# Batch 0's key-value products in four 128x32 tiles instead of two of 128x64

## The chip, the cores and the metric

The kernel runs on one core of one Trainium2 chip. The metric is the device time of one execution in microseconds (us); less is better. TensorE is called PE here, as in the profile, and its weight loads PEld; VectorE is DVE, ScalarE ACT, GpSimd POOL and SyncE SP.

## The reference

Two blocks follow each other. The first is a linear attention with a polynomial feature map: 4 batches, 4 heads, 1088 tokens, 32 channels a head, float32.

```python
phi(x)[i*8+j] = (S1 @ x)[i] * (S2 @ x)[j]          # 64 features from 32 channels
kv  = sum over tokens of phi(k) outer v            # 64 x 32, for each batch and head
z   = sum over tokens of phi(k)                    # 64
out = (phi(q) @ kv) / (phi(q) @ z + 1e-6)
```

Its output, transposed to 4352 tokens by 128 channels, goes through `gelu(x @ w_in) @ w_out` with 2048 hidden channels (exact gelu). The change touches `kv` and `z` of the first batch alone.

## The kernel before

**Staging.** The attention of batch 0 is computed first and alone, in a prologue of about 16 us. From then on PE works on the two large products of the second block (`hidden`, L735, and `project` / `two_products`, L872 and L821), 8 chunks of 512 tokens and a last one of 256 for the remainders, and the attention of batches 1 to 3 is put between them at fixed steps. Every engine executes its instructions in the order of the program text: the last lines of the kernel chain each instruction to the one before it on the same engine.

**The prologue around the change.** A batch has 1024 main tokens, worked on as 8 sets of 128 (one token to a partition), and a remainder of 64. Heads are handled as two pairs: `c` is the pair, `r` the head within it. `key_features` (L395) computes the features of the keys: products into PSUM (L390), a copy by ACT (L403, L406), the outer product by DVE (L407), one quarter of it by POOL (L404). `widen_v` (L353, POOL) copies the values beside a column of ones, so that one product gives `kv` and `z`: 33 columns. `expand_products` (L557) computes the sketches of the queries on PE, ACT copies half of them (L564) and DVE multiplies (L569, two instructions).

Then come the functions of the change. `kv_first(ps, r, tokens)` sums the products of the main tokens of head `r` of both pairs into one PSUM bank, `kv_first_rem` adds the remainder. In both, the stationary operand is the 64 features of one head over 128 tokens, and the moving operand the 33 columns of the values: the head of pair `c` writes PSUM partitions `64c` to `64c+63`. A matmul in float32 is two passes, and each pass is one record of PE and one of PEld in the trace.

On PE the order is:

```python
kv_first(kv_bank, 0, (0, 1, 4, 5))      # L434, 8 matmuls, 16 records
key_turn_rem(0, banks[1], by_act)       # L341, transpose of the remainder's keys; ACT copies it (kT_rem, L343)
kv_first(kv_bank, 0, (2, 3, 6, 7))      # L434, 16 records
key_features_rem(0, banks[1])           # L416, waits for kT_rem; ACT copies (a_rem, L420), DVE multiplies (k_p_rem, L421)
kv_first(kv_bank, 1)                    # L434, 32 records
kv_first_rem(kv_bank)                   # L440, 8 records, waits for k_p_rem
```

After these, PE transposes the queries of chunk 1 (L341, into `w_ps`), ACT copies the bank to `kz` (L941) and the transposed queries to `qT` (L948), and PE computes the numerators and denominators (L670) from `kz`. On ACT two steps of a weight's conversion (`bits_low` L263, `bits_r` L287) lie between `a_rem` and `kz`; on DVE the two multiplications of L569 lie ahead of `k_p_rem`, and the weight's conversion (L276 to L300) behind it.

Batches 1 to 3 sum `kv` in another form (`kv_product`, L445): the 32 values of a head over 128 tokens are stationary, the 64 features moving, and the four heads write four groups of 32 PSUM partitions. `z_sum` uses the same line with a tile of ones (32 columns) as the stationary operand.

Of the kernel before, what the change touches and what calls it, by code (L numbers as in the profile page):

```python
# [16 lines left out]
def kernel(  # L17
# [18 lines left out]
    pe, dve, act, pool, sp = nc.tensor, nc.vector, nc.scalar, nc.gpsimd, nc.sync  # L36
    B, H, S, D = q.shape
    R = S1.shape[0]
    F = R * R
# [3 lines left out]
    NP = H // 2  # L43
# [7 lines left out]
    C = D + 1  # L51
# [185 lines left out]
    v_rem_aug = [big.tile([128, H, D if b else 2 * D], FP, name=f"v_rem_aug{b}") for b in range(B)]  # L237
# [4 lines left out]
    v_aug = [att.tile([128, NP, J, 2 * D], FP, name="sums") for r in range(2)]  # L242
# [107 lines left out]
    kT, k_p, k_p_rem = {}, {}, {}  # L350
# [74 lines left out]
    def flat(features):  # L425
        return features.rearrange("p i j -> p (i j)")

    def kv_first(ps, r, tokens=range(J)):

        for i in tokens:  # L430

            ch, t, one = i // 4, i // 2 % 2, i % 2
            for c in range(NP):
                pe.matmul(ps[c * F:(c + 1) * F, r * 2 * D:r * 2 * D + C], lhsT=flat(k_p[0, r][:, t, c * 4 + ch * 2 + one]),  # L434
                          rhs=v_aug[r][:, c, i, :C], start=(r == 0 and i == 0), stop=False, skip_group_check=True)

    def kv_first_rem(ps):
        for r in range(2):
            for c in range(NP):
                pe.matmul(ps[c * F:(c + 1) * F, r * 2 * D:r * 2 * D + C], lhsT=flat(k_p_rem[0][:, 2 * c + r]),  # L440
                          rhs=v_rem_aug[0][:, 2 * c + r, :C], start=False, stop=True, skip_group_check=True)

    def kv_product(ps, lhsT, features, h, part, start=False, stop=False):

# [464 lines left out]
    r = Rounding(SR)  # L909
# [15 lines left out]
    for i in range(2):  # L925
        query_features(0, i)
    kv_bank = out_bank()
    kv_first(kv_bank, 0, (0, 1, 4, 5))
    key_turn_rem(0, banks[1], by_act)
    kv_first(kv_bank, 0, (2, 3, 6, 7))  # L930
    key_features_rem(0, banks[1])
    kv_first(kv_bank, 1)
    kv_first_rem(kv_bank)
    w_in = [Rounding(w) for w in w_in_sb[:2]]
    w_in[0].low_words()
# [167 lines left out]
    for n in range(3, NCHUNK):  # L1103

        t = (n - 1) * NF
# [160 lines left out]
```

## Time and profile before

| what | value |
|---|---|
| median of 3 runs | 259.04 us (258.95 to 259.43) |
| the profiled execution's own time | 259.29 us |
| its span | 257.5 us |
| PE busy | 253.3 us, 98% of the span, 2333 records |
| PEld / DVE / ACT / POOL busy | 135.0 / 151.7 / 114.4 / 164.1 us |
| granted PE clock | 1.00 |
| L434, 64 records | 2.4 us busy |
| L440, 8 records | 0.4 us busy |

A row of the trace gives the start, the duration and the engine, then line, operation, output tile and input tiles, the tile of the array that a matmul uses (`128*64` is 128 rows by 64 columns, the number of columns being that of the stationary operand), the shape of what is written, and the number of records. Of several matmuls in a row the duration is from the first start to the last end; one record of 33 columns lasts about 0.22 us from start to end, but the next begins long before that.

### The profile page before, as it was taken

The numbers are of one execution on the slowest core, as the hardware profiler recorded it, in microseconds if no ns is written. First come the engines' busy times: TensorE is split into PE (matmuls) and PEld (weight loads), VectorE is DVE, ScalarE is ACT, GpSimd is POOL, SyncE is SP. The second block draws the span as 40 slices with busy tenths as digits, with TensorE's granted clock in tenths as the row PEclk, the third lists the DMA queues.
The fourth block names the chain that finished last, engine by engine and source line by source line (L and its number), as shares of the span: only waits on it lengthen the run. The fifth ranks groups of instructions, "written<-read, shape, count | busy, mean of one in ns | idle before, by whom it ended". The sixth has DMA issues, their size and how long they took to land.

```text
span 257.5 us, 5763 instructions
## 1 busy us (share of the span) xinstructions
PE 253.3 (98%) x2333; PEld 135.0 (52%) x2333; DVE 151.7 (59%) x317; ACT 114.4 (44%) x221; POOL 164.1 (64%) x173
## 2 busy tenths in 40 slices
PE   8999999999999999999999999999999999999995
PEld 6856444355444545444444455455544444445794
DVE  3886879969698987580178976399307000700330
ACT  3685767433635333533335332523444334433442
POOL 3503016799968788587758775787758777877300
PEclk9999999999999999999999999999999999999999
DMA  6479848820000101101000002000200200020020
GB/s 208 136 221 368 179 105 210 224 47 10 3 0 13 30 1 23 20 12 31 3 0 3 0 10 36 1 1 3 41 3 7 37 0 1 7 36 0 3 41 20
DMA packets 29082, 13.48 MB, mean 52 GB/s; under 512 B 21888, under 2 KB 27264, under 8 KB 29056
## 3 DMA queue, kind: packets, MB, share of 16 engines
q1 hardware_dynamic: 28624, 12.79, 20.2%
q8 instruction: 18, 0.29, 0.5%
q10 hardware_dynamic: 432, 0.33, 0.4%
q14 instruction: 8, 0.07, 0.1%
HBM read 10.88 MB, written 2.23 MB: 51 GB/s over the span
## 4 chain that ended last, share of the span: by engine, by line
PE 98%; DVE 1%; issue 0%; ACT 0%; DVEq 0%
PE h_ps L735 45%; PE o_ps L821 33%; PE o_ps L872 5%; PE w_ps L869 3%; PE w_ps L445 1%; PE w_ps L592 1%; PE w_ps L904 1%; PE w_ps L647 1%; PE o_ps L434 1%; PE h_ps L751 1%; PE w_ps L989 1%; PE w_ps L557 0%; PE w_ps L670 0%; DVE x_tok L693 0%; PE h_ps L341 0%; PE w_ps L341 0%
## 5 line engine op out<-in xcount | busy, mean ns | idle before, releaser
L735 PE MATMUL h_ps<-xT,w_in 128*64 128x512 f32 (+3 forms) x514 | 136.8, 576 | 0.0
L742 ACT ACTIVATE block<-h_ps 128x512 f32<-128x512 f32 (+1 forms) x128 | 73.0, 571 | 117.3 <-PE h_ps L735 115.3
L735 PEld LDWEIGHTS h_ps<-xT,w_in 128*64 128x64 f32 (+1 forms) x514 | 41.7, 142 | 30.6 <-issue 11.9
L821 PE MATMUL o_ps<-block,w_out 128*64 128x256 f32 x224 | 57.5, 379 | 0.0
L786 POOL TENSOR_TENSOR bits_low<-block 128x512 f32<-128x512 f32 x28 | 36.1, 1290 | 27.6 <-ACT block L742 27.6
L821 PEld LDWEIGHTS o_ps<-block,w_out 128*64 128x64 f32 x224 | 30.5, 137 | 38.1 <-issue 27.6
L787 POOL TENSOR_TENSOR bits_a<-block 128x512 f32<-128x512 f32 x28 | 35.7, 1276 | 11.8 <-ACT block L742 11.6
L836 DVE COPY sums<-o_ps 64x256 f32<-64x256 f32 x8 | 3.3, 417 | 60.6 <-PE o_ps L821 60.6
L789 POOL TENSOR_TENSOR bits_m<-block,bits_e 128x512 f32<-128x512 f32 x28 | 36.0, 1287 | 2.2
L788 POOL TENSOR_TENSOR bits_e<-bits_a,block 128x512 f32<-128x512 f32 x28 | 36.0, 1286 | 2.2
L821 PE MATMUL o_ps<-block,small 128*64 128x256 f32 x112 | 28.8, 379 | 0.0
L821 PE MATMUL o_ps<-bits_a,small 128*64 128x256 f32 x112 | 28.8, 379 | 0.0
L821 PE MATMUL o_ps<-bits_low,small 128*64 128x256 f32 x112 | 28.8, 379 | 0.0
L821 PE MATMUL o_ps<-bits_m,w_out 128*64 128x256 f32 x112 | 28.7, 379 | 0.0
L821 PEld LDWEIGHTS o_ps<-block,small 128*64 128x64 f32 x112 | 15.2, 137 | 17.9 <-issue 10.8
L821 PE MATMUL o_ps<-bits_e,small 128*64 128x256 f32 x112 | 17.0, 383 | 0.0
L872 PE MATMUL o_ps<-g,w_out 128*128 128x512 f32 (+1 forms) x34 | 16.5, 572 | 0.0
L821 PEld LDWEIGHTS o_ps<-bits_m,w_out 128*64 128x64 f32 x112 | 15.3, 137 | 0.0
L821 PEld LDWEIGHTS o_ps<-bits_a,small 128*64 128x64 f32 x112 | 15.2, 137 | 0.0
L821 PEld LDWEIGHTS o_ps<-bits_low,small 128*64 128x64 f32 x112 | 15.2, 137 | 0.0
L604 DVE STREAM_TRANSPOSE w_ps<-w_ps 128x512 f32<-128x512 f32 (+1 forms) x7 | 4.8, 687 | 17.1 <-ACT xT L658 12.7
L821 PEld LDWEIGHTS o_ps<-bits_e,small 128*64 128x64 f32 x112 | 7.6, 137 | 10.6 <-issue 8.8
(197 smaller groups left out, 303.3 us busy)
## 6 DMA issues: line engine op xcount, KB each, us to landing
block<-in_moe_w_in_dram SPq DMA_DIRECT2D x3, 512.0 KB, 9.9
block<-in_moe_w_out_dram SPq DMA_DIRECT2D x3, 512.0 KB, 10.4
k<-in_k_dram SPq DMA_DIRECT2D x12, 128.0 KB, 2.8
v<-in_v_dram SPq DMA_DIRECT2D x12, 128.0 KB, 3.1
q<-in_q_dram SPq DMA_DIRECT2D x24, 64.0 KB, 2.6
out_dram<-oT SPq DMA_DIRECT2D x21, 64.0 KB, 2.2
q_first<-in_q_dram SPq DMA_DIRECT2D x2, 256.0 KB, 3.9
v<-in_v_dram SPq DMA_DIRECT2D x2, 256.0 KB, 4.5
```

The source lines that it names most:

```text
L434: pe.matmul(ps[c * F:(c + 1) * F, r * 2 * D:r * 2 * D + C], lhsT=flat(k_p[0, r][:, t, c * 4 + ch * 2 + one]), rhs=v_aug[r][:, c, i, :C], s ...
L604: dve.transpose(out=tok, in_=ps[:, :, :H2])
L735: pe.matmul(ps[rows, :W], lhsT=w[:, rows], rhs=xT[n][:, :W], start=True, stop=True)
L742: act.activation(out=g_of[n, fi][:, :W], in_=ps[:, :W], func=ACT.Gelu)
L786: pool.tensor_sub(out=s[3], in0=a11, in1=a21)
L787: pool.tensor_add(out=s[1], in0=a21, in1=a22)
L788: pool.tensor_sub(out=s[2], in0=s[1], in1=a11)
L789: pool.tensor_sub(out=s[4], in0=a12, in1=s[2])
L821: pe.matmul(acc[n][bank][half * 64:(half + 1) * 64, col:col + HW], lhsT=fixed, rhs=moving, start=opens and e == 0 and name in "4715", stop ...
L836: dve.tensor_copy(out=N[lo, 0, one], in_=a0[lo, one])
L869: pe.matmul(o_of[n][i][:, :128], lhsT=g[:, i * 128:(i + 1) * 128], rhs=w_tile(w_out_sb, fi), start=first, stop=final)
L872: pe.matmul(o_of[n][:, cols], lhsT=w_tile(w_out_sb, fi), rhs=g[:, cols], start=first, stop=final)
```

## The change

Each matmul of `kv_first` and `kv_first_rem` is split in two. A new function `kv_quarters` loops over the pair `c` and over `half`: 32 of a head's 64 features are the stationary operand, the moving operand is the same 33 columns, and the output goes to PSUM partitions `64c + 32*half` and the 31 behind. So 36 matmuls of 128x64 become 72 of 128x32. What is computed, the bank, the accumulation and the order of the calls stay as they are. No instruction of another engine is added, removed or moved, and the places where PE waits for another engine are the same; all lines behind the new function are numbered 5 higher, and its matmuls all stand at L433.

```diff
+    def kv_quarters(ps, r, features, values, start, stop):
+
+        for c in range(NP):
+            for half in range(2):
+                rows = slice(c * F + half * F // 2, c * F + (half + 1) * F // 2)
+                pe.matmul(ps[rows, r * 2 * D:r * 2 * D + C], lhsT=flat(features(c))[:, half * F // 2:(half + 1) * F // 2],
+                          rhs=values(c), start=start, stop=stop, skip_group_check=True)
+
     def kv_first(ps, r, tokens=range(J)):
 
         for i in tokens:
 
             ch, t, one = i // 4, i // 2 % 2, i % 2
-            for c in range(NP):
-                pe.matmul(ps[c * F:(c + 1) * F, r * 2 * D:r * 2 * D + C], lhsT=flat(k_p[0, r][:, t, c * 4 + ch * 2 + one]),
-                          rhs=v_aug[r][:, c, i, :C], start=(r == 0 and i == 0), stop=False, skip_group_check=True)
+            kv_quarters(ps, r, lambda c: k_p[0, r][:, t, c * 4 + ch * 2 + one], lambda c: v_aug[r][:, c, i, :C],
+                        r == 0 and i == 0, False)
 
     def kv_first_rem(ps):
         for r in range(2):
-            for c in range(NP):
-                pe.matmul(ps[c * F:(c + 1) * F, r * 2 * D:r * 2 * D + C], lhsT=flat(k_p_rem[0][:, 2 * c + r]),
-                          rhs=v_rem_aug[0][:, 2 * c + r, :C], start=False, stop=True, skip_group_check=True)
+            kv_quarters(ps, r, lambda c: k_p_rem[0][:, 2 * c + r], lambda c: v_rem_aug[0][:, 2 * c + r, :C], False, True)
```

## The prediction

> **What bounds the kernel now.** I read the page's chain first, then the chain in the stretch of the change (8 to 12.5 us), then the timeline of that stretch by engine, and last the rows of the tile shapes. The page's chain by engine, and its pieces in the stretch (start, us, what):
>
> ```profile
> PE 98%; DVE 1%; issue 0%; ACT 0%; DVEq 0%
> ```
>
> ```profile
> 8.31 0.59 PE o_ps L434 x16
> 8.90 0.26 PE o_ps L341
> 9.16 0.59 PE o_ps L434 x16
> 9.75 0.22 PE o_ps L416 x4
> 9.97 0.91 PE o_ps L434 x32
> 10.88 0.35 PE o_ps L440 x8
> ```
>
> PE ends nearly everything, and the chain puts 0.59 + 0.59 + 0.91 + 0.35 = 2.44 us of it on the matmuls that change. Taken at its word, faster matmuls here shorten the kernel by what they save. The chain goes back from each step to the instruction ahead on PE where it sees no wait, so the timeline of the same stretch must say whether PE could have begun earlier:
>
> ```profile
> 8.34 1.07 ACT L564 COPY A_sb<-w_ps 128x512 f32<-128x512 f32 x2 [0.80 <-PE w_ps L557]
> 8.84 0.33 PE L341 MATMUL o_ps<-ident,k_rem 128*128 128x128 f32 x1
> 8.96 1.28 DVE L569 TENSOR_TENSOR q_pT<-A_sb,w_ps 128x512 f32<-128x512 f32 x2
> 9.30 0.28 ACT L343 COPY kT_rem<-o_ps 128x128 f32<-128x128 f32 x1
> 9.64 0.34 PE L416 MATMUL o_ps<-S,kT_rem 128*64 128x64 f32 x4
> 10.24 0.42 DVE L421 TENSOR_TENSOR k_p_rem<-a_rem,o_ps 128x256 f32<-128x256 f32 x1
> 10.80 0.43 PE L440 MATMUL o_ps<-v_rem_aug,k_p_rem 128*64 128x33 f32 x8
> 10.96 0.51 ACT L287 ACTIVATE bits_r<-bits_e,below 128x256 uint32<-128x256 uint32 x1 [0.42 <-DVE bits_e L276]
> 11.16 0.66 PE L341 MATMUL w_ps<-ident,q_first 128*128 128x128 f32 x4
> 11.38 0.20 ACT L941 COPY kz<-o_ps 128x66 f32<-128x66 f32 x1
> 11.74 0.67 PE L670 MATMUL h_ps<-kz,q_pT 64*64 64x33 f32 x32
> ```
>
> Two places are pinned by others. L416 begins at 9.64, 0.06 us after ACT's `kT_rem` ends (9.58); ACT takes that copy up only when L564 is through, though its input was ready at 9.17 (8.84 + 0.33). L440 begins at 10.80, 0.14 us after DVE's `k_p_rem` ends (10.66), and DVE had no gap before it: L569 runs from 8.96 to 10.24. L564 hangs on L557, ahead of the change. So PE reaches L440 little before it may start, and the matmuls of L434 are hidden, nearly without slack, beside ACT and DVE.
>
> **The pace of each shape.** Starts overlap, so a record's price is (duration of the group less one record) over the records less one.
>
> ```profile
> 8.25 0.66 PE L434 MATMUL o_ps<-sums,k_p 128*64 128x33 f32 x16
> 55.11 1.08 PE L445 MATMUL w_ps<-k_p,v 128*32 128x64 f32 x64
> L434 PEld LDWEIGHTS o_ps<-sums,k_p x64: 132/138/138, 8.2 to 10.6; 128*64 128x64 f32 x64
> L445 PEld LDWEIGHTS w_ps<-k_p,v x192: 110/110/110, 55.1 to 154.1; 128*32 128x32 f32 x192
> ```
>
> L434: (0.66 - 0.22)/15 = 29 ns; L445: (1.08 - 0.22)/63 = 13.7 ns. Over one round of the tiles, two in L434 and four in L445, that is 58 and 55 ns. A weight load grows by 28 ns from 32 to 64 columns, so about 0.85 ns a column: 64 columns are 54 ns, 32 are 27. Streaming costs the same (matmuls of 64, 128 and 256 columns last 219, 273 and 379 ns): 33 columns are 28 ns, 64 are 54. So a round of L434 is its 64-column weight load (54) and 4 ns more; a round of L445 is its 64-column stream. The changed form has the small side of both, 32 columns to load and 33 to stream: 28 plus 4 is 32 ns a round of four tiles, 8 ns a record. The shape is in no row. Its bounds: 7 ns (28 over four tiles, nothing more) and 29 ns, L434's own price, if four tiles help nothing. L445 is the nearest row, the same tile, but its 13.7 ns are set by a stream twice as long, so I take 8 and keep 13.7 as the cautious value.
>
> **The sum on PE.** 72 records at 29 ns are 2.09 us; 144 at 8 ns are 1.15 us, 0.94 us less. Where it goes:
>
> - First and second call (16 records each, now 32): 0.46 us become 0.26, twice. The transpose L341 ends 0.2 us earlier, but `kT_rem` waits for ACT's L564, so L416 stays at 9.64. Gain on the path: nothing; PE idles before L416.
> - Third call (32 records, now 64): 0.93 us become 0.51. The switch from the 64-column tiles of L416 to 32-column tiles is new. Where the array changes its tile the trace has 0.15 us between the last start and the next (L440 to L341: 11.01 to 11.16) and 0.20 (L341 to L670), against 0.05 from L416 to L434 within one tile form. So the call begins at about 9.95 and its last record at 9.95 + 0.50 = 10.45; `k_p_rem` still ends at 10.66. Gain: nothing. The cover is DVE's work; were it gone, 0.35 us would be gained here.
> - L440 (8 records, now 16): it starts at 10.80 as before. Its last record starts at 10.80 + 15 x 8 ns = 10.92 instead of 11.01 (10.80 + 0.43 - 0.22): 0.09 us earlier. PE's transposes of the queries follow at 11.07, and L670 at 11.65. It can take that: `kz` is pinned at 11.38 by ACT's L287 (weight conversion, behind DVE's L276) and ends at 11.58, and about 0.05 us later L670 could start. So 0.09 of at most 0.12 us comes through. From L670 on PE, ACT and DVE follow it, and PE stays full to the end.
>
> The sum is -0.09 us on the execution of 259.29, that is 259.20; the median lies 0.25 lower, so 258.95. Two costs I take at nothing: the issue of 144 more PE instructions (no idle time of PE between 8 and 12.5 us is put down to issue), and a moving operand read twice as often (L445 streams into four tiles at once).
>
> Written with the record's price p, the last record of L440 starts at 9.1 us + 144p when nothing hides it (8.25, then 0.15 + 0.26 for the first switch and the transpose, 0.15 for the second switch, 0.31 for L416 and the switch behind it): level with before at p = 13.2 ns, 0.2% (0.52 us, about what a measurement of this kernel can tell from no change) later at 16.8 ns. At L445's 13.7 ns it is +0.07 us.
>
> [...]
>
> **Rivals.**
>
> - *Slower: the price is per record and four tiles share nothing.* Every record at 29 ns: 9.1 + 144 x 0.029 = 13.28 against 11.01, +2.3 us, 261.2. It decides from 16.8 ns on. Against it: L445's 13.7 and L670's 14.5. For it: no row shows less than 12 ns for a long run. [...] Chance of anything past 16.8 ns: 0.14.
> - *A floor of 13 to 16 ns a record*, which L445 and L670 may both be showing: then the second call delays L416, slack is used up, and the result is 0 to +0.5 us, 259.0 to 259.5. Chance 0.22.
> - *Faster: the chain at its word*, all 0.94 us arrive: 258.1. It needs L416 and L440 not to wait for ACT and DVE, against the ends at 9.58 and 10.66. Chance 0.06.
> - *PE's clock drops* because PE idles for some 0.5 us before L416 and 0.3 before L440. The clock is granted at 1.00 everywhere, past PE's idle moments in the first 5 us too; a drop to half for 3 us would cost 1.5 us, 260.5. Chance 0.03.
> - The change does what it says: the compiled order has 72 matmuls of 32 columns, and the waits stand where they stood.
>
> **The numbers.** The forecast (absorbed, 0.12 us gained to level) has what is left, 0.55. Faster by over 0.2%: 0.06, the chain at its word. Slower by over 0.2%: 0.14 + 0.03 = 0.17. Within: 0.55 + 0.22 = 0.77. The range goes from the most that L670's wait for `kz` allows (258.92) and the spread of the runs below it, 258.7, to the floor's upper end, 259.6; outside lie the two slow rivals and the chain's gain.
>
> **What would show it.** In the profile after: L433's rounds of four at about 32 ns, so a group of 64 records lasts near 0.72 us (0.50 + 0.22) instead of 1.08; L416 still at 9.64 and L440 at 10.80, with PE idle before each and DVE `k_p_rem` unmoved; L670 at 11.65. Wrong, if L416 or L440 moves later (a price above 13 ns), if either moves earlier (my pins are none), or if the clock falls.

## The result, and the profile after

The changed kernel is slower: 261.83 us median of 9 runs (261.16 to 263.14) against 259.51 us (258.95 to 261.46) of 9 runs of the kernel before beside them. The ratio is 1.0088, 95% interval 1.006 to 1.0116. Forecast were 258.95 us and a range to 259.6. The profiled execution took 261.75 us with a span of 260.0 (before 259.29 and 257.5), so 2.5 us are to be found in its trace.

The page of the changed kernel: the span, the row of engines, the chain by engine, and the DMA queue that carries instructions (packets, MB, share).

```profile
span 260.0 us, 5907 instructions
PE 255.3 (98%) x2405; PEld 135.7 (52%) x2405; DVE 151.8 (58%) x317; ACT 114.4 (44%) x221; POOL 164.1 (63%) x173
PE 97%; DVE 1%; ACT 0%; issue 0%
q8 instruction: 19, 0.31, 0.5%
```

The row of q8 on the page before:

```profile
q8 instruction: 18, 0.29, 0.5%
```

There are 72 more records on PE and 72 more on PEld, 144 instructions, and one more packet of code. Nothing here explains 2.5 us: PE is the chain as it was. The timeline of the changed kernel, in the stretch up to the second L562, shows (start, us, engine, line, operation, tiles, shape, records, idle before and what ended it):

```profile
6.56 1.08 PE L390 MATMUL o_ps<-S,kT 64*64 64x32 f32 x32
8.42 2.01 PE L562 MATMUL w_ps<-qT,Srep 32*64 32x256 f32 x32
11.77 0.34 PE L416 MATMUL o_ps<-S,kT_rem 128*64 128x64 f32 x4 [0.30 <-ACT kT_rem L343]
12.03 0.77 PE L433 MATMUL o_ps<-sums,k_p 128*32 128x33 f32 x64
12.93 0.33 PE L433 MATMUL o_ps<-v_rem_aug,k_p_rem 128*32 128x33 f32 x16
13.20 0.66 PE L341 MATMUL w_ps<-ident,q_first 128*128 128x128 f32 x4
14.85 1.55 PE L562 MATMUL w_ps<-qT,Srep 32*64 32x256 f32 x32
15.71 0.23 PEld L562 LDWEIGHTS w_ps<-qT,Srep 32*64 32x64 f32 x14 [0.25 <-issue]
```

The first two rows had been, before:

```profile
5.93 0.67 PE L390 MATMUL o_ps<-S,kT 64*64 64x32 f32 x32
7.00 1.32 PE L557 MATMUL w_ps<-qT,Srep 32*64 32x256 f32 x32
```

Matched record by record, the lag of PE behind the kernel before is 0.62 us at L390, 2.13 us at L416 (11.77 against 9.64), 2.04 us at the queries' L341 (13.20 against 11.16), 2.47 us behind the second L562, and it stays there to the end of the kernel.

- So the lag of 2.13 us is there before the third call begins, on matmuls that the change did not touch: L390 takes 1.08 us instead of 0.67, L562 2.01 instead of 1.32. That is PE at about half pace: in a later run, at a granted clock of half, 32 records of L675 took 1.08 us instead of 0.67. The trace's clock record, which lists when the granted clock changed, has full clock from 10.35 us on here and from 5.03 us on before. (The clock column of the page says 1.00 for both: durations have to be read.)
- The part that the change does touch gains: from L416 to L341 the lag falls by 0.09 us, the forecast gain.
- In the second L562 PE waits for nothing that the profile shows (the last row, "issue"), and the lag grows by 0.43 us, from 2.04 to 2.47.

Two causes, it seems, of which only the small one lies behind the change. The experiments turned that round.

### The profile page after: what moved, and what is told of

The parts are those of the page before. It is cut to its first block, busy times and chain, and to the rows that moved or that the text cites. A ratio compares the mean times of both kernels' runs of the same rounds, so it can differ in the third digit from the quotient of the medians.

```text
span 260.0 us, 5907 instructions
## 1 busy us (share of the span) xinstructions
PE 255.3 (98%) x2405; PEld 135.7 (52%) x2405; DVE 151.8 (58%) x317; ACT 114.4 (44%) x221; POOL 164.1 (63%) x173
## 3 DMA queue, kind: packets, MB, share of 16 engines
HBM read 10.88 MB, written 2.23 MB: 50 GB/s over the span
## 4 chain that ended last, share of the span: by engine, by line
PE 97%; DVE 1%; ACT 0%; issue 0%
PE h_ps L740 45%; PE o_ps L826 33%; PE o_ps L877 5%; PE w_ps L874 3%; PE w_ps L450 1%; PE w_ps L597 1%; PE w_ps L909 1%; PE w_ps L652 1%; PE w_ps L562 1%; PE h_ps L756 1%; PE w_ps L994 1%; DVE q_pT L574 0%; PE w_ps L675 0%; PE h_ps L341 0%; PE o_ps L390 0%; PE h_ps L390 0%
## 6 DMA issues: line engine op xcount, KB each, us to landing
block<-in_moe_w_out_dram SPq DMA_DIRECT2D x3, 512.0 KB, 10.5
```

## The experiments

Four theories were set against each other. Theory A: the length of the program decides, wherever the instructions lie, when PE gets to full pace. Theory T (in some expectations B): the four-tile matmuls themselves cost more than their records show, or bring the late pace. Theory C: chance, which differs from run to run. Theory F, raised in two of the first four expectations and spelled out after those runs: PE waits for its own code. "Stand" below is the time from the start of one PE or PEld record to the start of the next, where PE stops without a wait that the profile shows. Record numbers run from 0 and count the records of PE, PEld and PE's sequencer (semaphore waits and drains, 32 in the whole kernel before) together, one for each instruction. They, and the times of the code packets on q8, are read from the trace's single records.

### 36 spare matmuls at the very end of the kernel before

```diff
+    spare = hidden_bank()
+    for i in range(36):
+        pe.matmul(spare[rows, :33], lhsT=zeros_128x32, rhs=zeros_128x33, start=True, stop=True)   # rows: 32 * (i % 4)
```

> The kernel before with 36 matmuls of 128x32 more (33 moving columns, zeros, into a spare bank) as the last work of PE, behind the last product; nothing in the first 250 us is changed. In the changed kernel PE ran at half pace up to 10.4 us (L390: 32 records in 1.08 us instead of 0.67), ahead of the first changed matmul, and in the kernel before only up to 5.0. Theory A (the length of PE's program, 144 instructions more, decides when PE gets to full pace): the half pace lasts past 6 us here too, L390's first 32 records take about 1.08 us, and the time is 261 to 262 us. Theory B (it hangs on the 32-column tiles at their place): L390 takes 0.67 us, 259.0 to 260.0 us. Theory C (chance of a run, no relation to the program): either, and it differs between the runs of one kernel by about 2 us.

Measured: 261.31 us (260.98 to 261.43) against 259.65, ratio 1.0068 [1.0042, 1.0094]. The sum looks like theory A's, the trace does not. Its timeline, early and at the end:

```profile
6.39 0.67 PE L390 MATMUL o_ps<-S,kT 64*64 64x32 f32 x32
254.85 0.83 PE L1232 MATMUL h_ps<-const-float32-0.0 128*32 128x33 f32 x72
```

Early PE is at full pace from 6.09 us, and its last products (L869) end only 0.6 us later than before. The other 1.4 us lie in the end. The last store lands in sixteen parts; fifteen of them have landed by 257.27 us, 2.0 us after the issue as before, and the sixteenth lands at 258.67, 3.4 us after it, with a code packet on q8 beside it (256.29 to 257.49 us). That the packet delays this part is argued, not shown; the trace with 256 spare matmuls below has the same picture (sixteenth part at 258.63 us, a packet up to 257.53). Theory A as a law of program length falls with this trace.

### Only the remainder in four tiles

```diff
 def kv_first: ... as before, two tiles of 128x64
 def kv_first_rem: kv_quarters(...)          # 4 matmuls become 8
```

> The change in the remainder's products alone (kv_first_rem, L440: 4 matmuls become 8, 16 PE instructions more); the main tokens as before. By the prediction's sum the step itself is worth -0.09 us, 259.4 beside a median of 259.5 of the kernel before. Theory A (length of PE's program): either a small shift of the moment of full pace, or none, since only 16 instructions are added; if every instruction counts alike, a ninth of the loss, +0.3 us. Theory B (the tiles): about a ninth of the loss too, or none. Theory C (chance): 259 or 261, differing between runs.

Measured: 259.39 us (258.9 to 259.89) against 259.65, ratio 0.9995 [0.9984, 1.0006]. This step is the one the forecast's 0.09 us came from; alone it is no difference that can be measured. In the profiled execution (259.89 us, 0.5 above this median) PE came early to L676 and stood there for 0.92 us, at record 449, going on 0.5 us later than PE had reached that number before (12.59 against 12.11):

```profile
10.54 0.33 PE L433 MATMUL o_ps<-v_rem_aug,k_p_rem 128*32 128x33 f32 x16
11.39 0.47 PE L676 MATMUL h_ps<-kz,q_pT 64*64 64x33 f32 x17
12.59 0.37 PE L676 MATMUL h_ps<-kz,q_pT 64*64 64x33 f32 x12 [0.73 <-issue]
```

### Only the first two calls in four tiles

```diff
 def kv_first(ps, r, tokens):
+    if r == 0: kv_quarters(...); continue    # r == 1 and the remainder as before
```

> The change in the first two calls of kv_first alone (head 0, 16 matmuls become 32, 64 PE instructions more); the third call and the remainder as before. By the prediction's sum the step is worth nothing on the path: 259.5. Theory A (length of PE's program): slow start as in the changed kernel if 64 instructions suffice, 261 to 262. Theory B (the tiles at the first call): slow start, 261 to 262. Theory C: differs between runs. Also: where PE stood still for 0.4 us at its record 705 (in L562), the still stand should come at the same record number, that is 64 records later in the text, if it is the fetch of PE's code.

Measured: 261.93 us (260.88 to 264.14), ratio 1.0105 [1.0052, 1.0159]. These two calls were forecast to bring nothing and cost nothing, as PE idles behind them. They carry 64 of the 144 instructions and a loss as large as the whole change's within the intervals (four runs alone, the profiled one the shortest of them). PE was at full pace from 5.47 us, so the late pace of the changed kernel's profile is not needed for a loss. PE stood 0.42 us at record 449 (the queries' L341 lags by 0.56 us) and 0.85 us at record 3265, at 156 us, far from the change; together 1.4 of the 1.6 us between the spans (259.1 and 257.5):

```profile
11.48 0.30 PE L452 MATMUL o_ps<-v_rem_aug,k_p_rem 128*64 128x33 f32 x2 [0.20 <-issue]
155.87 0.98 PE L604 MATMUL w_ps<-qT,S_abc 64*32 64x256 f32 x22
157.32 0.63 PE L604 MATMUL w_ps<-qT,S_abc 64*32 64x256 f32 x5 [0.47 <-issue]
```

449 and 3265 are 256k - 63 (k = 2 and 13). The stand that the expectation looked for at record 705 did not come: with only 64 more instructions PE gets there at 19.21 us, long after the packet that landed at 13.72. That gave theory F.

### The change, with 36 matmuls left out far behind it

```diff
 in kv_sum (batches 1 to 3):
-    for i in range(J):
+    for i in range({1: J, 2: J - 2, 3: 1}[b]):
```

> The changed kernel with 36 matmuls fewer later on: batch 2's key-value sum leaves out 2 of its 8 sets of tokens and batch 3's 7 of 8 (L450), so PE's program is as long as before the change. The 72 records left out are worth 72 x 13.7 ns = 1.0 us. Theory A (length of PE's program): full pace from 5 us as before, 258.0 to 259.0 us. Theory B (the tiles): the slow start stays, 260.5 to 261.5 us. Theory C: differs between runs. The stand of 0.4 us in L562 stays by both, if it is the fetch of PE's code.

Measured: 261.19 us (260.24 to 262.61), ratio 1.0069 [1.0046, 1.0093], though the program is as long as before and the 72 records left out are worth 72 x 13.7 ns = 1.0 us. Theory A falls for good. This profile is the clearest of all, as PE has full pace early (5.27 us):

```profile
10.05 0.55 PE L433 MATMUL o_ps<-sums,k_p 128*32 128x33 f32 x38
11.41 0.41 PE L433 MATMUL o_ps<-sums,k_p 128*32 128x33 f32 x26 [0.81 <-issue]
11.63 0.35 PE L433 MATMUL o_ps<-v_rem_aug,k_p_rem 128*32 128x33 f32 x16
13.57 0.86 PE L562 MATMUL w_ps<-qT,Srep 32*64 32x256 f32 x17
15.37 0.69 PE L562 MATMUL w_ps<-qT,Srep 32*64 32x256 f32 x15 [0.94 <-issue]
```

PE stands inside a run of equal matmuls, with nothing to wait for: 1.01 us at record 449, 1.32 us at record 705, each counted from start to start (the bracket counts from the modelled end of the last matmul). The busy time of each engine in two stretches says the same (from:to, length, PE, PEld, DVE, ACT, POOL with records, clock, DMA share, GB/s), first for this kernel, then for the kernel before:

```profile
8.00:12.00 4.00, 2.90 (x171) 2.02 (x153) 3.85 (x9) 2.27 (x6) 1.51 (x3) 1.00 0.29 104
12.00:16.00 4.00, 3.06 (x101) 2.10 (x101) 2.00 (x11) 1.88 (x6) 0.78 (x3) 1.00 0.42 99
```

```profile
8.00:12.00 4.00, 4.00 (x113) 3.38 (x101) 3.77 (x9) 2.53 (x8) 1.66 (x3) 1.00 0.27 100
12.00:16.00 4.00, 3.79 (x106) 2.94 (x100) 2.94 (x14) 3.06 (x9) 0.80 (x3) 1.00 0.39 105
```

PE loses 1.10 us and 0.73 us of busy time. On the DMA side, code packets run on q8 from 8.95 to 9.88 and from 12.75 to 14.03 us; PE goes on at 11.41 and 15.37, 1.5 and 1.3 us after each has landed. The lag behind the kernel before is 2.07 us at the matmul where PE goes on; less the 1.0 us left out later, 1.1 remain, which is the difference of the spans (258.6 against 257.5).

### Half of batch 0's tokens: the four-tile form without more instructions

```diff
-    kv_first(kv_bank, 0, (0, 1, 4, 5))  ...  (2, 3, 6, 7)  ...  kv_first(kv_bank, 1)
+    kv_first(kv_bank, 0, (0, 1))        ...  (2, 3)        ...  kv_first(kv_bank, 1, (0, 1, 4, 5))
     kv_first_rem: for r in range(1)
```

> The changed kernel's form, 128x32 tiles in all four calls, over half of the tokens (head 0: 0, 1 and 2, 3; head 1: 0, 1, 4, 5; the remainder of head 0 alone), so 36 matmuls in this stage as before the change, not 72. It leaves out half of batch 0's keys and values. Theory F (PE waits for its own code: the records of PE stand still at 449 and 705, that is every 256 records of weight load and matmul, until about 1.4 us after a fetch of 16 KB of code has landed): with the old count the ends of the blocks lie where they lay before the change, no stand at 705 and at most 0.5 us at 449: 259.2 to 260.0 us. Theory T (the small tiles themselves are slow, or disturb what follows): 260.7 us or more. If the late full pace of PE (10.4 us in the changed kernel's trace) was its cause: no forecast, the moment differs from run to run.

Measured: 259.43 us (259.16 to 259.87) against 259.54, ratio 1.0 [0.9988, 1.0011]: 36 matmuls of 128x32 for 36 of 128x64. No stand. Theory T falls: the form, at the old count, costs nothing that can be measured.

```profile
9.63 0.34 PE L416 MATMUL o_ps<-S,kT_rem 128*64 128x64 f32 x4 [0.48 <-ACT kT_rem L343]
9.90 0.46 PE L433 MATMUL o_ps<-sums,k_p 128*32 128x33 f32 x32
10.80 0.27 PE L433 MATMUL o_ps<-v_rem_aug,k_p_rem 128*32 128x33 f32 x8 [0.44 <-DVE k_p_rem L421]
11.00 0.66 PE L341 MATMUL w_ps<-ident,q_first 128*128 128x128 f32 x4
```

These rows also test the prediction's pins: L416 at 9.63 and the remainder at 10.80, to 0.01 us where they were, PE idle before each.

### The kernel before, with 36 idle matmuls behind the remainder

```diff
     kv_first_rem(kv_bank)
+    for i in range(36):
+        pe.matmul(kv_bank[rows, 256:289], lhsT=zeros_128x32, rhs=zeros_128x33, start=True, stop=True)   # columns nobody reads
```

> The kernel before, its products as they were, and 36 matmuls of 128x32 with 33 columns of zeros more behind kv_first_rem, into unused columns of the bank: as many instructions more as the change adds, in the same stretch. Their own time is 72 x 8.6 ns and two changes of tile, 0.9 us: 260.5 us if only work counts. Theory F (code): 144 instructions more ahead of L670 bring the ends of the blocks forward; stands at records 449 and 705 together of 1 to 2 us, 261.2 to 262.0 us.

Measured: 262.01 us (261.72 to 262.88) against 259.54, ratio 1.0113 [1.0087, 1.0138]. More instructions bring the loss with the two-tile form untouched. The idle matmuls take time of their own (0.9 us by the expectation's estimate, which gave 260.5 us if only work counts); the result is 1.5 us above that, and the stands are 0.53 us at record 449 and 1.05 us at record 705:

```profile
12.25 0.58 PE L936 MATMUL o_ps<-const-float32-0.0 128*32 128x33 f32 x42 [0.34 <-issue]
14.42 0.86 PE L557 MATMUL w_ps<-qT,Srep 32*64 32x256 f32 x17
15.95 0.69 PE L557 MATMUL w_ps<-qT,Srep 32*64 32x256 f32 x15 [0.67 <-issue]
```

### 256 spare matmuls at the end

The edit is the first one with 256 for 36: 1024 instructions with nothing to wait for.

> The kernel before and 256 matmuls of 128x32 with 33 columns of zeros as PE's last work (1024 instructions): the pace of code by itself, where no load runs. Theory F: a block of 256 instructions (64 of these matmuls, 128 records) takes about 3.9 us, 31 ns a record, with stands of some 2.5 us every 256 trace records; 12 to 16 us longer, 271 to 275 us. If code is no limit: 512 records at 8.6 ns, 4.4 us, some 2 of them beside the last store: about 262 us.

Measured: 270.13 us (270.0 to 270.27), ratio 1.0418 [1.0397, 1.0439].

```profile
254.65 2.08 PE L1232 MATMUL h_ps<-const-float32-0.0 128*32 128x33 f32 x181
259.05 1.28 PE L1232 MATMUL h_ps<-const-float32-0.0 128*32 128x33 f32 x128 [2.32 <-issue]
262.50 1.98 PE L1232 MATMUL h_ps<-const-float32-0.0 128*32 128x33 f32 x128 [2.17 <-issue]
266.23 1.31 PE L1232 MATMUL h_ps<-const-float32-0.0 128*32 128x33 f32 x75 [1.74 <-issue]
```

The period of the supply, by itself: each full stretch is 128 PE records, with their 128 weight loads 256 instructions, and the stretches begin 3.45 and 3.73 us apart, though the first of them executes in 1.28 us. That is 27 to 29 ns a PE record. Packets land at 257.53, 261.13 and 265.05; PE goes on 1.52, 1.37 and 1.18 us later. (The third row lasts 1.98 us because the clock fell to 0.50 at 261.33 us, during the second stand.) The total is 0.9 us under the range that theory F had forecast: its 3.9 us a block were too many here.

### The changed kernel once more

> The changed kernel once more, for a second trace of it. Theory F: if PE gets to full pace at 5 to 6 us in this run, the stands are about 1.0 us at record 449 and 1.3 us at 705 (as in the kernel with 36 matmuls fewer later on), and the time is 261.2 to 262 all the same, since what comes sooner to the end of a block waits longer there. If the late pace was the cause in the first trace: a run with early full pace takes 259.5 us.

Measured: 262.53 us (261.83 to 263.22), ratio 1.0125 [1.0088, 1.0162]. Full pace comes at 4.65 us this time, so the late one of the first profile does not belong to the change in every execution; the stand at record 449 is 1.88 us (10.06 to 11.94), and during it, at 11.48 us, the clock falls to half, up to 18.30 us. The forecast 1.3 us at record 705 did not come, since PE at half clock gets there only at 16.25 us, and the time is above the forecast 261.2 to 262. Theory C falls as well: the eleven runs of the changed kernel all took 261.16 us or more, and of the runs of the kernel before all but one (261.46) took 260.25 or less. Timeline, then windows:

```profile
9.71 0.55 PE L433 MATMUL o_ps<-sums,k_p 128*32 128x33 f32 x38
11.94 0.60 PE L433 MATMUL o_ps<-sums,k_p 128*32 128x33 f32 x26 [1.68 <-issue]
12.69 1.11 PE L341 MATMUL w_ps<-ident,q_first 128*128 128x128 f32 x4
```

```profile
10.00:15.00 5.00, 3.32 (x122) 2.81 (x112) 1.77 (x8) 1.99 (x6) 0.79 (x3) 0.65 0.26 69
15.00:20.00 5.00, 4.77 (x73) 3.40 (x66) 3.19 (x15) 2.32 (x8) 0.00 (x0) 0.67 0.95 283
```

This execution is 263.22 us: a stand can cost its own length and a spell of half clock as well, which may be why the changed kernel's runs spread over 2 us and the kernel before's mostly over 0.8. The runs' mean granted clocks speak for it: of the nine runs of the changed kernel in the result, the two longest (262.53 and 263.14 us) have 0.986 and the other seven 0.998 or more, and a half clock for 6.83 of 261 us makes 0.987.

### A weight's load held back, in both kernels

The code packets travel beside the loads of the prologue (with 36 fewer later, 132 packets of q1 and one of q8 moved between 8.5 and 10.5 us). If those delay the first packet, a freer DMA should bring it earlier.

```diff
+            pool.memset(to[0:1, 0:1], 0)      # ahead of load_w_in(1), which then waits for POOL
```

> The changed kernel, with the load of the second quarter-megabyte piece of w_in (used from about 12.3 us on) held back by a gate on POOL until about 8.9 us, so that the DMA engines are freer from 7 to 9 us. What is computed stays the same. Theory F, with the addition that the first fetch of code waits behind the loads of the input (it began at 9.0 to 10.2 us in the traces, 1.5 to 3 us after record 193, where in the tail without loads it began 1.1 us after a block's end): the fetch begins at 8.0 to 9.0 us, the stand at record 449 shrinks from 1.0 to 1.9 us to 0.2 to 1.0, that at 705 comes earlier and keeps about its size, and the time falls by 0.3 to 0.9 us from the changed kernel's, 260.9 to 261.5 us. If the loads do not hold the fetch: it begins at 9.0 us or later as before, and the time stays at 261.8 or is worse by a later weight.

> The kernel before with the same load held back. Its trace shows no stand at 449 (reached at 12.1 us, some 0.2 us after the code was there). If some of its runs stand there after all, an earlier fetch takes the spread of its runs (258.8 to 260.2 us) away and the median falls to 259.0 to 259.3; if not, 259.3 to 259.8, the same as before.

Measured: the changed kernel 261.87 us (260.83 to 262.91) against 259.77, ratio 1.0077 [1.0044, 1.011]; the kernel before 259.72 (258.95 to 261.49), ratio 1.0009 [0.9988, 1.003]. In the latter the first packet went at 8.40 to 9.36 us instead of 9.49 to 10.45. The changed kernel's profile happened to have the late full pace again (10.29 us), its first packet at 9.31 to 10.26, and it stood 0.43 us at record 705. Nothing was won; what fixes the packet's start stays open.

## Why the prediction was wrong

**The cause.** PE's code comes in blocks of 256 instructions, as far as the stands (at records 449, 705 and 3265) and the packets of q8 (16 KB each, 18 for the 4698 records of the kernel before) show it. The change's 144 more all lie ahead of record 705. In the text before, records 449 and 705 stood in L670 and in the chunk's next L670, and PE reached them at 12.11 and 19.12 us, 1.7 and 5.2 us after the packets that landed at 10.45 and 13.91 us; by the 1.2 to 1.5 us between landing and use in the other runs, that is about when the second block became usable and long after the third had. In the changed text they stand in the third call and in the second L562, a matmul that PE had reached at 13.30 us before. The rows of the kernel before:

```profile
12.81 1.12 PE L557 MATMUL w_ps<-qT,Srep 32*64 32x256 f32 x32
18.58 1.14 PE L670 MATMUL w_ps<-kz,q_pT 64*64 64x33 f32 x64
```

The third block is usable at 15.37 to 15.95 us in every one of these traces:

| kernel | full pace from | stand at 449 | stand at 705 | goes on behind 705 at | that matmul's lag |
|---|---|---|---|---|---|
| changed | 10.35 us | none (449 at 12.36) | 0.38 us | 15.71 us | 2.41 us |
| changed, 36 fewer later | 5.27 us | 1.01 us | 1.32 us | 15.37 us | 2.07 us |
| before, 36 idle more | 5.87 us | 0.53 us | 1.05 us | 15.95 us | 2.65 us |

Whether PE comes there at half pace or at full pace and waits, it goes on at about the same time, so the late full pace in the first profile seems to have cost little by itself: it used up time in which PE would have stood. 15.37 to 15.95 less 13.30 is the loss: 2.07 to 2.65 us, against 2.5 between the spans and 2.32 between the medians.

The stands are all at record 256k - 63, and each ended after a packet's landing. In this kernel's large products the ends of the blocks cost nothing that shows: in the trace of the kernel before the packets that start at 50.13 and 57.22 us leave no stand, and from record 449 on every record 256k - 63 begins at most 0.11 us after the one ahead of it. Where 256 instructions execute in 1.28 us, as with the 256 spare matmuls, the next stand is 2.17 us (by the bracket).

**Point by point.**

- *The two costs taken at nothing.* The failed step is "the issue of 144 more PE instructions (no idle time of PE between 8 and 12.5 us is put down to issue)": taken at 0, it measured 2.07 to 2.65 us, as PE waits for code at a place where it had not waited. The argument looked only for a stand that was there already. The trace held the number: code packets landing at 10.45 and 13.91 us, and the same matmul at 13.30. With the 1.2 to 1.5 us found since between landing and use, 13.91 + 1.3 - 13.30 = 1.9 us of loss could have been worked out. The other cost taken at nothing, the moving operand read twice as often, is nothing to speak of: a record takes 8.7 ns where the forecast had 8.
- *First and second call: "Gain on the path: nothing".* Right for the gain, and incomplete: these two alone measured +1.0% through their 64 instructions.
- *The pace of the four-tile form, 8 ns a record, 32 ns a round.* Right: 64 records in 0.77 us are (0.77 - 0.22)/63 = 8.7 ns, 35 ns a round; forecast were 0.72 us.
- *The pins by ACT and DVE.* Right, by the half-token run: 9.63 and 10.80 us. In the changed kernel's own profile L416 and the remainder begin at 11.77 and 12.93 us, not because of a record's price but because ACT and DVE come later too: 0.06 and 0.14 us behind the ends of `kT_rem` and `k_p_rem`, as before.
- *The sum of -0.09 us.* Right in the stage itself (the lag falls from 2.13 to 2.04 us); too small to show in the run with the remainder alone.
- *The slower rival, 261.2 us, at 29 ns a record.* Its time lay near the result, its mechanism was not there: the records go at 8.7 ns, which rules out the floor of 13 to 16 ns as well. (The 14.5 ns of L670 that speak against this rival are (0.67 - 0.22)/31, from its row.) That the supply of code gives 27 to 29 ns a record is a coincidence of size.
- *The clock rival.* A spell at half clock did come in one profile of the changed kernel, during its stand of 1.88 us, and it lasted 6.83 us, where the rival's sum has 3 us, which no row of the trace before gave. The idle moments that it was argued from did not bring one in the other profiles. The argument against it read the page's clock of 1.00 in the first 5 us as measured; the clock record begins only at 5.03 us.

**What stays open.** What sets the start of the first code packet (8.4 to 10.2 us in these traces); why full pace came at 10.3 us in two of the three profiles of the changed kernel (one of the two with the load held back) and in no other, for which the last section has a part of the answer; and the last 1.4 us of the run with 36 spare matmuls at the end. The run with the remainder alone is the best of the changed forms, and it equals the kernel before.

## What to carry to other kernels

A matmul of small tiles costs its instructions too, and here they had a price where they were executed faster than their code arrived (256 in 1.28 us against one packet every 3.45 to 3.96 us): count the instructions per us of the dense stretches, look at when the packets of the instruction queue land, and find the instruction at each block's end. Idle time put down to "issue" in the middle of a run of equal matmuls was the sign (0.81 and 0.94 us with 36 fewer later). Behind long matmuls, where the packets left no stand here, I estimate that twice the instructions are free (no run tried it there); in this prologue of short ones 144 more cost 2.3 us between the medians, and the 64 of the first two calls, in the shadow of other engines, cost as much within the intervals.

## What the runs showed of the hardware

- **Supply of code to PE.** A float32 matmul here is four instructions (36 more are 144 more records), and q8 brings a packet of 16 KB for each 256: 18, 19 and 22 packets for the 4666, 4810 and 5690 records of PE and PEld before, after and with the 256 spare matmuls. In a dense stretch 256 instructions arrive every 3.45 to 3.96 us (3.45 and 3.73 with the 256 spare matmuls, 11.41 to 15.37 with 36 fewer later): about 1.1 to 1.3 us from PE's going on to the next packet, 0.95 to 1.4 us of transfer, 1.2 to 1.5 us until PE goes on.
- **Half clock from a stand.** During a stand of 1.88 us the clock fell to half, for 6.83 us; with the 256 spare matmuls it fell to half at 261.33 us, during the second stand (2.17 us by the bracket). At half clock 32 records of L675 took 1.08 us instead of 0.67, as those of L390 did in the late first stretch.
- **The clock changes on a grid of 3.413 us.** In all eleven profiles with a clock record, full or half clock lasts a whole number of such steps from one change to the next: 252.586 us (74), 249.173 (73), 256.000 (75), 6.827 (2). Six steps were read for the busy time of PE: behind the two with 1.91 us (8.06 to 11.47 us in the changed kernel once more) and 1.28 us (257.91 to 261.33 with the 256 spare matmuls) the clock fell; behind those with 2.32 and 2.47 us (8.68 to 15.51 us with 36 fewer later, one stand in each), 2.23 us (254.50 to 257.91 with the 256 spare) and 2.00 us (255.05 to 258.46 with 36 idle more) it stayed. So in these six the clock fell behind the least busy steps; no run varied the busy time alone.
- **The moment of full pace varies by itself.** It came between 4.2 and 6.1 us in nine profiles, and at 10.3 us in two. In the clock records it goes with the place of the first matmul on that grid: the first matmul starts at 0.77 us in every profile; in the nine the first grid point behind it lies at 0.80 to 2.68 us and full pace comes one step later, while in the two late ones a grid point lies just ahead of it, at 0.05 and 0.11 us, and full pace comes three steps behind that point. Why the step from 3.5 to 6.9 us did not bring it there, and whether the change has any part in where the grid lies, is not shown. The granted clock of the page, 1.00 from 0 to 5 us, doesn't show this first stretch at half pace.
